# Linear attention into a gated MLP: the first pair's v from GpSimd in half precision, and the sixth tile stored in halves

## The chip, the cores and the metric

The kernel runs on one core of one Trainium2 chip. The metric is the device time of one execution in microseconds (us), lower is better; the time of a kernel is the median of several executions. A profile shows one more execution with the start and length of every instruction. Five instruction streams run side by side on the core: TensorE (PE, matmuls; PEld is its weight load), VectorE (DVE), ScalarE (ACT), GpSimd (POOL) and SyncE (SP). A DMA is issued from one of these streams and carried out by 16 DMA engines that all streams share. In the profile a DMA issued from SP or ACT shows as queue q1 or q10 ("hardware_dynamic") and one issued from POOL as queue q0 ("software_dynamic"). POOL's can convert the type on the way.

## What is computed

A linear attention over 8 batches, 8 heads, 576 rows and 64 columns, an RMS norm per head, and then a two-layer MLP with a sigmoid gate on the 4608 rows of 512:

```python
kv  = np.einsum('bhsd,bhse->bhde', k, v)
out = np.einsum('bhsd,bhde->bhse', q, kv)
rms = np.sqrt(np.mean(out * out, axis=-1, keepdims=True) + 1e-06)
x   = (out / rms * g_norm).transpose(0, 2, 1, 3).reshape(4608, 512)
h   = x @ w_in                                # 512 -> 2048
g   = h * (1.0 / (1.0 + np.exp(-1.702 * h)))
y   = g @ w_out                               # 2048 -> 512
```

Inputs and output are float32. On the chip the matmuls run on float16.

## The kernel before

The 4608 rows go through the MLP as nine tiles of 512: tile t below 8 holds the first 512 rows of batch t, and tile 8 the 64 rows that each batch has over. While the MLP of one tile runs on PE, the attention of a later batch is worked in between. From the second tile on both layers of the MLP are done with seven products where eight would be usual (`SevenIn`, `Seven`), with sums formed on DVE.

Nothing reorders the program: each engine runs its instructions in the order in which the code emits them, and a semaphore wait on the first instruction of a stream holds all that are behind it.

**The opening** is what the change touches. Batch 0 is worked by head pairs c = 0 to 3 (`NPAIR` = 4). A pair has q, k and v of two heads, laid as 96 partitions by 768 values (`early_src`). The first pair is loaded on SP's list in float32 into staging tiles named `qf` (lines 154 to 161: first k, then q, then v) and cast to float16 into `kraw`, `qraw` and `vbuf`: q on ACT (L860), k and v on DVE (L861, L862). Pairs 1 to 3 are loaded on POOL's list by `early_load` (L91), which converts to float16 on the way, nine loads in the order q, k, v per pair (L187 to L189). Behind them on POOL's list stand eight loads of `moe_w_in` by `load_w_in` (L180; lines 190 to 197): three pieces of 512 columns and 128 rows for the first four column blocks, then columns 8 and 9 (in blocks of 128) for all rows, then the fourth piece of the first four blocks, and so on; then `moe_w_out` (L206) and batch 1.

POOL uses eight DMA semaphores in turn (they read DMASW0 to DMASW7 in the listings below; SP's and ACT's are DMAHW0 to DMAHW7). A load on POOL's list can only be issued when the load eight places ahead of it has landed, since it reuses that one's semaphore.

On PE the opening reads: 12 matmuls on zeros (`busy(12)`, L869), the transposes of the first pair's q (L439, `a0.q(0)`), 2 matmuls on zeros, the k-v product of the first pair (L261, `a0.kv(0)`), its output product (L307), and so on pair by pair; L384 is the sum for the norm (`ss`), L325 and L386 are its square and root on ACT, L394 scales on DVE. Then come the first hidden blocks (L478, `d0.mm`): the first four column blocks with rows 0, 1 and 2, then column blocks 8 and 9 with rows 0 to 2, then the fourth row piece for all six.

**The stores.** A finished tile lies in `osbs[t]` (128 partitions, 4 by 512). For the tiles named in `HALVED`, `place` (L696) issues a store from SP for each half when the half is full; tiles 6 and 7 are stored whole at the end of `layers` (L801, `store`, L852). Tile 8 is stored in pieces (L743).

```python
        elif self.t in HALVED and j == 1 - i:
            store(self.t, 2 * i, 2 * i + 2)
```

Of the kernel before, what the change touches and what calls it, by code (L numbers as in the profile page):

```python
# [8 lines left out]
F32 = mybir.dt.float32  # L9
# [3 lines left out]
P = 128  # L13
# [3 lines left out]
def kernel(  # L17
# [10 lines left out]
    nc = tc.nc  # L28
# [14 lines left out]
    PE_ = 96  # L43
# [6 lines left out]
    stage = ctx.enter_context(tc.tile_pool(name="stage", bufs=4))  # L50
# [18 lines left out]
    vbuf = const.tile([P, NPAIR, 2 * NJ * D], F16)  # L69
# [17 lines left out]
    def early_src(n, b, c0, c1):  # L87
        return srcs[n][b, 2 * c0 : 2 * c1].rearrange("h (p j) d -> p h (j d)", j=NJ)

    def early_load(n, b, c0, c1):  # L90
        nc.gpsimd.dma_start(  # L91
            out=raw[n][0:PE_, c0:c1, :].rearrange("p c (l x) -> p (c l) x", l=2),
            in_=early_src(n, b, c0, c1),
        )
# [57 lines left out]
            )  # L152

    first = {}
    for n in "kqv":
        if n != "q":
            rows = stage.tile([P, 6, 2 * P], F32, name="qf", tag="qf", bufs=2)
            rows = rows.rearrange("p h x -> p (h x)")[0:PE_]
        first[n] = rows[:, (n == "q") * 2 * NJ * D :][:, 0 : 2 * NJ * D]
        dst, src = first[n].rearrange("p (h x) -> p h x", h=2), early_src(n, 0, 0, 1)  # L160
        nc.sync.dma_start(out=dst, in_=src)
# [17 lines left out]
    def load_w_in(f0, f1, k0=0, k1=KO):  # L179
# [4 lines left out]
            ),  # L184
        )

    for c in range(1, NPAIR):  # L187
        for n in "qkv":
            early_load(n, 0, c, c + 1)  # L189
# [429 lines left out]
    class Seven:  # L619
# [60 lines left out]
        def place(self, name, mo, with_, i, j):  # L680
# [9 lines left out]
            if self.t == B:  # L690
# [3 lines left out]
                else:  # L694
                    store_rest(2 + mo, j * HN, (j + 1) * HN)
            elif self.t in HALVED and j == 1 - i:  # L696
                store(self.t, 2 * i, 2 * i + 2)
# [34 lines left out]
    def store_rest(mo, n0, n1):  # L732
        osb = osbs[B]
        for g in range(2):
            rows = out[(2 * mo + g) * S : (2 * mo + g + 1) * S, n0:n1]
            if 2 * mo + g < EARLY:
                p0 = SM % PE_
                rows = rows[bass.DynSlice(NJ * p0 + SM // PE_, R, step=NJ), :]
            else:
                rows = rows[SM:S, :]  # L740
            late = mo == 2 and n0 > 0
            queue = nc.gpsimd if mo == 0 or late else (nc.sync, nc.scalar)[g]
            queue.dma_start(out=rows, in_=osb[g * R : (g + 1) * R, mo, n0:n1])  # L743
# [43 lines left out]
    def layers(t, units1, units2):  # L787
# [11 lines left out]
        else:  # L799
            project_all(hid.gT, units2)  # L800
        if EARLY <= t < B and t not in HALVED:  # L801
            store(t, 0, J)
# [11 lines left out]
    def project_all(gT, units):  # L814

        os = {}

        def project(mo, fo):
            if fo == 0:
                pool, tag = (ps_h, "hT") if mo < 2 else (ps_o, "o")  # L820
                os[mo] = pool.tile([P, DM], F32, name="o", tag=tag)
            nc.tensor.matmul(  # L822
                os[mo],
                gT[:, fo, mo * P : (mo + 1) * P],
                w_out_sb[:, fo, :],
                start=(fo == 0),
                stop=(fo == FO - 1),
            )
            if fo == FO - 1:
                copy = nc.scalar.copy if mo % 2 else nc.vector.tensor_copy  # L830
                copy(osbs[0][:, mo, :], os[mo])

        steps = [(mo, 4 * i + k) for i in range(3) for mo in range(4) for k in range(4)]
        steps += [(mo, fo) for fo in (12, 13) for mo in range(4)]
        steps += [(mo, 14 + k) for mo in range(4) for k in range(2)]
        for n, (mo, fo) in enumerate(steps):
            project(mo, fo)
            for u in units.get(n, ()):
                u()
# [11 lines left out]
    def store(t, j0, j1):  # L851
        nc.sync.dma_start(  # L852
            out=out[t * S : t * S + SM, :].rearrange("(p j) m -> p j m", j=J)[:, j0:j1],
            in_=osbs[t][:, j0:j1],
        )
# [3 lines left out]

    nc.scalar.copy(qraw[0:PE_, 0, :], first["q"])  # L860
    nc.vector.tensor_copy(kraw[0:PE_, 0, :], first["k"])  # L861
    nc.vector.tensor_copy(vbuf[0:PE_, 0, :], first["v"])  # L862


    idle_ps = ps_h.tile([P, SM], F32, name="idle", tag="hT")
# [110 lines left out]
    def plan(t):  # L976
        return SECOND if t < EARLY else LATER if t < B - 1 else LAST_TWO

    HALVED = (2, 3, 4, 5)
    live = {0: a0}  # L980

    def start(b):
# [136 lines left out]
```

## Time and profile before

| | before |
|---|---|
| median of 3 executions | 258.72 us (258.68 to 258.73) |
| the profiled execution | 258.06 us |
| its span (first to last instruction) | 256.3 us |
| granted TensorE clock | 0.999 |
| POOL's queue (q0) | 18.31 MB, 37648 packets |
| SP's queue (q1) | 16.29 MB, 30624 packets |

The span is the part of the execution that the profile shows; 1.8 us of the profiled execution lie around it. MB counts what a DMA writes, so a load that converts float32 to float16 reads twice that. A line of the timeline gives the start in us, the length in us, the engine, the line of the code, the operation, output and input, and how many were merged; in brackets stands the idle time before it and what ended it. A line of the chain of waits gives start, length and what ran then. A DMA line of POOL or SP in the timeline is the time of issuing it, and not that of its data.

### The profile page before, as it was taken

What the parts mean: (1) busy time and instruction counts of PE and PEld (TensorE: products, weight loads), DVE (VectorE), ACT (ScalarE), POOL (GpSimd) and SP (SyncE); (2) the same over time, 40 slices, a digit from 0 to 9 for tenths busy, and PEclk for the clock granted to TensorE, in tenths of its full rate; (3) what the DMA queues carried; (4) which work ended last, traced back from release to release, by engine and by line L of the source; (5) the groups of instructions that cost most, each with busy time, mean ns of one, the idle gap of its engine ahead of it and who ended that gap; (6) DMA issues with size and microseconds to landing.
All of it is one profiled execution on the core that took longest, in us unless ns stands there. A gap on an engine that the chain in (4) does not pass through costs nothing.

```text
span 256.3 us, 6351 instructions
## 1 busy us (share of the span) xinstructions
PE 250.1 (98%) x2596; PEld 203.5 (79%) x2596; DVE 194.3 (76%) x341; ACT 176.9 (69%) x322; POOL 57.5 (22%) x94
## 2 busy tenths in 40 slices
PE   8899999999999999999999999999999999999994
PEld 2444544888888888888888888888888888888883
DVE  2557675999958895989588867986799687857872
ACT  3468826978759885988598958895788569537800
POOL 8872255404080103301340143000000000000013
PEclk9999999999999999999999999999999999999999
DMA  7999999999999989998999799909500430012005
GB/s 179 198 199 206 204 203 197 190 173 150 141 163 220 133 118 177 209 271 114 216 170 130 90 232 145 154 4 145 195 4 0 100 148 3 0 75 91 0 22 146
DMA packets 68703, 35.33 MB, mean 138 GB/s; under 512 B 37986, under 2 KB 66274, under 8 KB 68418
## 3 DMA queue, kind: packets, MB, share of 16 engines
q0 software_dynamic: 37648, 18.31, 55.5%
q1 hardware_dynamic: 30624, 16.29, 28.0%
q8 instruction: 20, 0.33, 0.5%
q10 hardware_dynamic: 402, 0.33, 0.4%
q14 instruction: 9, 0.07, 0.1%
HBM read 36.70 MB, written 9.44 MB: 180 GB/s over the span
## 4 chain that ended last, share of the span: by engine, by line
PE 92%; POOL 3%; DMA 3%; issue 0%; DVE 0%
PE o L709 39%; PE h L589 38%; PE o L822 5%; PE hT L478 4%; DMA w_in_sb<-in_moe_w_in_dram 3%; PE kvp L248 2%; PE outR L337 1%; POOL qraw L91 1%; POOL kraw L91 1%; POOL vbuf L91 1%; PE ss L384 1%; POOL w_in_sb L180 1%; PE q L459 0%; PE kvp L261 0%; PE outT L307 0%
## 5 line engine op out<-in xcount | busy, mean ns | idle before, releaser
L566 ACT ACTIVATE gT<-h 128x512 f16<-128x512 f32 x96 | 52.3, 601 | 5.7 <-PE h L589 5.7
L589 PEld LDWEIGHTS <-ws 128*128 128x128 f16 x512 | 50.1, 98 | 5.9
L709 PEld LDWEIGHTS <-gS 128*128 128x128 f16 x512 | 49.0, 98 | 6.2 <-DVE gS L641 0.3
L589 PE MATMUL h<-xS,ws 128*128 128x256 f16 x384 | 52.2, 273 | 0.0
L709 PE MATMUL o<-tw,gS 128*128 128x256 f16 x384 | 45.6, 273 | 0.0
L589 PEld LDWEIGHTS <-w_in_sb 128*128 128x128 f16 x384 | 37.5, 98 | 4.7
L709 PEld LDWEIGHTS <-gT 128*128 128x128 f16 x384 | 37.6, 98 | 4.3
L709 PE MATMUL o<-w_out_sb,gT 128*128 128x256 f16 x256 | 31.4, 273 | 0.0
L589 PE MATMUL h<-xT,w_in_sb 128*128 128x256 f16 x224 | 31.1, 272 | 0.0
L603 DVE TENSOR_TENSOR h<-h,s 128x512 f32<-128x512 f32 x32 | 22.3, 697 | 4.4 <-PE h L589 2.8
L605 DVE TENSOR_TENSOR s<-h,s 128x512 f32<-128x512 f32 x32 | 22.1, 691 | 4.3 <-PE h L589 3.5
L686 DVE TENSOR_TENSOR osb<-o,qf 128x512 f32<-128x512 f32 (+1 forms) x25 | 16.7, 667 | 11.2 <-PE o L709 11.1
L743 POOL DMA_DIRECT2D out_dram<-osb x6 | 3.2, 538 | 93.3 <-DVE osb L686 93.3
L641 DVE TENSOR_TENSOR gS<-gT 128x512 f16<-128x512 f16 (+2 forms) x32 | 21.3, 684 | 0.6 <-ACT gT L566 0.6
L566 ACT ACTIVATE gT<-s 128x512 f16<-128x512 f32 x32 | 19.8, 628 | 2.8 <-DVE s L605 2.8
L535 DVE COPY s<-h 128x512 f32<-128x512 f32 x19 | 13.0, 685 | 8.1 <-PE h L589 8.0
L589 PE MATMUL h<-xS,w_in_sb 128*128 128x256 f16 x128 | 18.9, 273 | 0.0
L353 DVE TENSOR_REDUCE sum<-sq 128x8 f32<-128x512 f16 x24 | 14.9, 678 | 4.7 <-ACT sq L347 4.7
L993 ACT ACT_TABLE_LOAD x14 | 18.0, 1283 | 0.2
L325 ACT ACTIVATE sq<-outT 128x512 f16<-128x512 f32 (+1 forms) x16 | 7.8, 493 | 14.8 <-PE outT L307 9.2
L115 POOL DMA_DIRECT2D kraw<-in_k_dram x7 | 6.0, 855 | 49.2 <-PE kvp L248 32.6
L535 ACT COPY h<-h 128x512 f32<-128x512 f32 x27 | 15.4, 577 | 2.1 <-PE h L589 1.8
(105 smaller groups left out, 365.4 us busy)
## 6 DMA issues: line engine op xcount, KB each, us to landing
out_dram<-osb SPq DMA_DIRECT2D x8, 512.0 KB, 5.6
kraw<-in_k_dram POOLq DMA_DIRECT2D x5, 512.0 KB, 6.1
vbuf<-in_v_dram POOLq DMA_DIRECT2D x5, 512.0 KB, 9.9
out_dram<-osb SPq DMA_DIRECT2D x2, 1024.0 KB, 4.8
qraw<-in_q_dram POOLq DMA_DIRECT2D x3, 512.0 KB, 11.0
qbuf<-in_q_dram POOLq DMA_DIRECT2D x3, 512.0 KB, 12.0
out_dram<-osb SPq DMA_DIRECT2D x6, 192.0 KB, 6.1
w_in_sb<-in_moe_w_in_dram POOLq DMA_DIRECT2D x2, 512.0 KB, 9.9
```

Of the source, the lines that this page charges most:

```text
L353: nc.vector.tensor_reduce(out=self.sum4[:, j, :], in_=self.o[j][1].rearrange("p (x d) -> p x d", d=D), op=ALU.add, axis=mybir.AxisListType.X,)
L478: nc.tensor.matmul(self.h[fo], w_in_sb[:, ko, fo * P : (fo + 1) * P], self.x[:, ko], start=(ko == 0), stop=(ko == KO - 1),)
L535: (nc.vector.tensor_copy if engine == "D" else nc.scalar.copy)(to, src)
L566: nc.scalar.activation(self.gT[:, to, n * TH : (n + 1) * TH], src, AFT.Gelu_apprx_sigmoid)
L589: nc.tensor.matmul(bank[name][:, a], w, x, start=(p in (1, 5) and a == 0 and k == 0), stop=(k == KH - 1), skip_group_check=True,)
L603: nc.vector.tensor_add(bank["z"], bank["x"], self.s5)
L605: nc.vector.tensor_add(self.s5, bank["x"], self.s5)
L641: op(s[:, n, lo], a, b)
L686: nc.vector.tensor_add(o, ps, self.kept[with_][:, m])
L709: nc.tensor.matmul(o, a, w, start=(p in (1, 2, 5) and i == 0 and (mo == 0 or split)), stop=(i == HF - 1), skip_group_check=True,)
L822: nc.tensor.matmul(os[mo], gT[:, fo, mo * P : (mo + 1) * P], w_out_sb[:, fo, :], start=(fo == 0), stop=(fo == FO - 1),)
L993: u2.setdefault(i, []).append(lambda: f(*args))
```

## The change

The first pair's v leaves SP's list and the float32 staging tile. It becomes the first load on POOL's list, which writes float16 straight into `vbuf`. The cast on DVE falls away. SP's list begins with two loads, k and q. All that stood on POOL's list stands one place further back. Apart from that, tile 6 joins the tiles that are stored in halves.

```diff
     first = {}
-    for n in "kqv":
-        if n != "q":
-            rows = stage.tile([P, 6, 2 * P], F32, name="qf", tag="qf", bufs=2)
-            rows = rows.rearrange("p h x -> p (h x)")[0:PE_]
+    rows = stage.tile([P, 6, 2 * P], F32, name="qf", tag="qf", bufs=2)
+    rows = rows.rearrange("p h x -> p (h x)")[0:PE_]
+    for n in "kq":
         first[n] = rows[:, (n == "q") * 2 * NJ * D :][:, 0 : 2 * NJ * D]
...
+    early_load("v", 0, 0, 1)
     for c in range(1, NPAIR):
         for n in "qkv":
             early_load(n, 0, c, c + 1)
...
     nc.vector.tensor_copy(kraw[0:PE_, 0, :], first["k"])
-    nc.vector.tensor_copy(vbuf[0:PE_, 0, :], first["v"])
...
-    HALVED = (2, 3, 4, 5)
+    HALVED = (2, 3, 4, 5, 6)
```

POOL's list from its first DMA to the first load of `moe_w_in`, before (the brackets name the semaphore that the instruction waits for):

```order
L91 DMA qraw<-in_q_dram 96x2x384
L91 DMA kraw<-in_k_dram 96x2x384
L91 DMA vbuf<-in_v_dram 96x2x384
L91 DMA qraw<-in_q_dram 96x2x384
L91 DMA kraw<-in_k_dram 96x2x384
L91 DMA vbuf<-in_v_dram 96x2x384
L91 DMA qraw<-in_q_dram 96x2x384
L91 DMA kraw<-in_k_dram 96x2x384
L91 DMA vbuf<-in_v_dram 96x2x384 [waits DMASW0_49]
L180 DMA w_in_sb<-in_moe_w_in_dram 128x512 [waits DMASW1_49]
```

The same place with the change:

```order
L91 DMA vbuf<-in_v_dram 96x2x384
L91 DMA qraw<-in_q_dram 96x2x384
L91 DMA kraw<-in_k_dram 96x2x384
L91 DMA vbuf<-in_v_dram 96x2x384
L91 DMA qraw<-in_q_dram 96x2x384
L91 DMA kraw<-in_k_dram 96x2x384
L91 DMA vbuf<-in_v_dram 96x2x384
L91 DMA qraw<-in_q_dram 96x2x384
L91 DMA kraw<-in_k_dram 96x2x384 [waits DMASW0_49]
L91 DMA vbuf<-in_v_dram 96x2x384 [waits DMASW1_49]
L179 DMA w_in_sb<-in_moe_w_in_dram 128x512 [waits DMASW2_49]
```

Each load has moved one place back and one semaphore on, so the load that it waits for is the same as before; the only new wait is that of the third pair's k for the new first load.

The end of SP's list, where the stores of tiles 6 and 7 stand behind the last transposes (the `x` in the names is the normed attention output of batch 7):

```order
-L373 DMA_TRANSPOSE xT<-x_3174 128x8x128 x2
-L852 DMA out_dram<-osb 128x2048 x2
+L373 DMA_TRANSPOSE xT<-x_3172 128x8x128 x2
+L852 DMA out_dram<-osb 128x1024 x2
+L852 DMA out_dram<-osb 128x2048
 L743 DMA out_dram<-osb 64x256 x5
```

One of the two whole stores has become two half stores; behind them stands what stood there before.

## The prediction

> **What bounds the kernel now.** I read the page first, then the chain of waits, then the timeline of the opening, and last the DMA queues in short windows.
>
> ```profile
> PE 250.1 (98%) x2596; PEld 203.5 (79%) x2596; DVE 194.3 (76%) x341; ACT 176.9 (69%) x322; POOL 57.5 (22%) x94
> PE 92%; POOL 3%; DMA 3%; issue 0%; DVE 0%
> ```
>
> PE is busy nearly all the span and makes up 92% of the chain that ended last. The change leaves PE's list as it is, so it can only move the moment from which PE runs without a gap. The chain in order of time shows that moment:
>
> ```profile
> 1.84 0.73 POOL qraw L91
> ...
> 6.99 0.62 POOL vbuf L91
> ...
> 9.85 6.81 DMA w_in_sb<-in_moe_w_in_dram
> 16.66 0.05 issue
> 16.70 4.49 PE hT L478 x20
> 21.20 0.12 PE outT L419 x4
> 21.31 6.91 PE hT L478 x32
> 28.22 1.08 PE o L822 x5
> ```
>
> From 16.70 us on it is PE without a break. Ahead of that stands one load of `moe_w_in`, columns 8 and 9, issued at 9.85 and landed at 16.66. The timeline shows who waits in the opening:
>
> ```profile
> 5.96 0.79 DVE L862 CAST vbuf<-qf 96x768 f16<-96x768 f32 x1 [1.09 <-DMA qf<-in_v_dram]
> 7.43 0.38 PE L261 MATMUL kv<-vbuf,kraw 96*64 96x64 f16 x12
> 11.74 0.45 PE L439 MATMUL q<-ident,qraw 96*64 96x96 f16 x12
> 12.09 0.59 ACT L325 ACTIVATE sq<-outT 128x512 f16<-128x512 f32 x1
> 12.68 0.38 PE L261 MATMUL kv<-vbuf,kraw 96*64 96x64 f16 x12 [0.50 <-DMA vbuf<-in_v_dram]
> 12.99 0.39 PE L384 MATMUL ss<-sq,ones 128*128 128x512 f16 x1
> 16.70 4.49 PE L478 MATMUL hT<-xT,w_in_sb 128*128 128x512 f16 x20 [0.25 <-DMA w_in_sb<-in_moe_w_in_dram]
> ```
>
> PE stands 0.50 us for the last pair's v and 0.25 us for columns 8 and 9. Both come through POOL's queue, so PE follows that queue: what shifts the queue shifts the end. That leaves the question of what paces the queue, issuing or data:
>
> ```profile
> 1.79 0.79 POOL L91 DMA_DIRECT2D qraw<-in_q_dram  x1
> qraw<-in_q_dram POOLq DMA_DIRECT2D x1, 144.0 KB, 4.8
> 6.92 0.69 POOL L91 DMA_DIRECT2D vbuf<-in_v_dram  x1
> vbuf<-in_v_dram POOLq DMA_DIRECT2D x1, 144.0 KB, 5.6
> GB/s 0 0 0 59 194 344 341 283 277 264 203 171 198 194 191 192 191 198 200 198 198 201 201 201 200 201 199 190 221 185 204 189 192 197 202 203 206 209 207 203
> ```
>
> The last number of a DMA row is the time from issue to landing. The first of POOL's nine loads lands at 1.79 + 4.8 = 6.6, the ninth at 6.92 + 5.6 = 12.5. They were issued (6.92 - 1.79) / 8 = 0.64 us apart and landed 5.9 / 8 = 0.74 apart, so the data set the pace. The row of GB/s cuts 0 to 20 us into 40 slices: from 2.5 us there is no slice in which the engines rest. The chain blames POOL's issuing for the time before 9.85, but its issues there run ahead of the data.
>
> **The change part by part.** *The first pair's v on the other queue.* Its data cost DMA time in either place. The queues in windows, in this order: 0 to 20 us (q1 alone), 1.6 to 4.0, 2.6 to 4.6, 4.0 to 5.2 (two rows), 6 to 12:
>
> ```profile
> q1 hardware_dynamic: 624, 0.88, 15.4%
> q1 hardware_dynamic: 422, 0.61, 88.5%
> q1 hardware_dynamic: 439, 0.62, 104.1%
> q1 hardware_dynamic: 199, 0.27, 78.9%
> q0 software_dynamic: 51, 0.04, 24.5%
> q0 software_dynamic: 1654, 1.18, 130.1%
> ```
>
> SP's three loads are 624 packets, 208 each. By 4.0 us 422 have gone, which is k and q; v fills most of 4.0 to 5.2. No packet of POOL's queue is seen in 1.6 to 4.0, nor up to 4.6; 51 go beside v's before 5.2, and from then POOL has the engines alone at 1654 / 6 = 276 packets per us. The 51 are worth 0.185 us, so POOL's queue stands as if it had begun at full pace at 5.015.
>
> With the change SP's data are through at about 4.0. POOL's queue has one more load; taking the same 208 packets, it costs 208 / 276 = 0.755 us (the spacing of landings above, 0.74, agrees). In float32 on SP's queue a load cost 208 / (439 / 2) = 0.95 us, and v in its own stretch 1.03 (1.2 less 0.185, rounded). If POOL's queue starts as soon as SP's is through, the next load begins at 4.0 + 0.755 = 4.755 in place of 5.015: everything behind is **0.26 us earlier**. With the mean of 0.95 for v it would be 0.19; both are the same step. From what start the sign turns: 5.015 - 0.755 = 4.26 us.
>
> Can the queue start at 4.0? Its first load is issued at 1.79, as the first of the changed list will be. Two other places bound the delay between issue and first packet, one with a quiet q1 and one with a busy one:
>
> ```profile
> 140.76 0.91 POOL L115 DMA_DIRECT2D kraw<-in_k_dram  x1 [9.80 <-PE kvp L248]
> q0 software_dynamic: 282, 0.14, 76.6%
> 98.71 0.88 POOL L115 DMA_DIRECT2D vbuf<-in_v_dram  x1
> q1 hardware_dynamic: 1343, 0.45, 108.8%
> q0 software_dynamic: 69, 0.04, 39.2%
> ```
>
> The first q0 row is 142 to 144 us (from 140.8 to 142 q0 has no row): the quiet delay is about 1.3 us. The other two are 98.7 to 101, where q1 alone moves data, and 101 to 102: behind a busy q1 the delay is over 2.3. In the opening it was 2.8 (1.79 to 4.6), q1 being busy all along. With 1.3 from the quiet place POOL could start at 3.1, before SP's two loads are through. I take 4.0 because the late starts go with a busy q1 at both places. As bounds I keep both ends: 4.65, if the start stays where it is, and, for the best, 4.0 with a faster mix, priced below.
>
> [...]
>
> *One more issue on POOL.* Each later load is issued one place later, about 0.64 us. It is hidden by the lag of 4.8 to 5.6 us between issue and landing, of which 1.3 is the quiet delay and 0.75 the load's own data. The wait for the load eight places ahead is unchanged. The one new wait, the third pair's k for the new first load, asks at about 6.9 for something landed by 6.3 at worst (next step).
>
> *The first pair's v itself.* Sent by 4.76, or by 5.4 from a start at 4.65. The first POOL load of before had its 208 packets out at about 5.2 + (208 - 51) / 276 = 5.8 and landed at 6.6, so 0.8 on top: 5.6 to 6.2. PE wants it at 7.43, behind the zero matmuls and q's transposes: at least 1.2 us of cover, cost nothing. Were the cover gone, PE would stand for the excess.
>
> *The cast on DVE* (0.79 us, 5.96 to 6.75) goes. Nothing on DVE behind it was late: its next work waits for PE, and k-v began at 7.43 by PE's own order. Worth nothing. SP's third issue goes too, and nothing behind it on SP's list belongs to the opening.
>
> *Tile 6 in halves.*
>
> ```profile
> 201.76 0.69 DVE L686 TENSOR_TENSOR osb<-o,qf 128x512 f32<-128x512 f32 x1 [0.66 <-PE o L709]
> 203.50 0.58 ACT L689 COPY osb<-o 128x512 f32<-128x512 f32 x1 [2.26 <-PE o L709]
> 204.11 25.01 SPq L852 DMA_DIRECT2D out_dram<-osb  x2
> 202.00:204.00 2.00, 2.00 (x21) 1.80 (x19) 1.45 (x4) 0.50 (x2) 0.00 (x0) 1.00 0.00 0
> ```
>
> The first half can leave at 202.5 in place of 204.1. In 202 to 204 the DMA share is 0.00, the transposes ahead on SP are over, and the next thing on SP is tile 7's store some 25 us later. Worth nothing.
>
> *From the queue to the end.* 0.26 earlier reaches the last pair's v (PE is free at 11.74 + 0.45 = 12.19, so up to 0.49 can be used), the norm sum at 12.99 (its square on ACT ends at 12.68: 0.31), and the wait at 16.70. Every later piece of `moe_w_in` moves with the same queue, and PE runs on unbroken. So the sum is -0.26: the profiled execution would go from 258.06 to 257.80. The median shown is 0.66 above that execution; I carry the difference over: 258.72 - 0.26 = **258.46**.
>
> **The rivals.**
>
> *The start stays at 4.65* (slower). POOL's first DMA needs 2.8 us by itself, whatever q1 does. From 4.65 to 5.2 the queue then sends 0.55 x 276 = 152 packets where 51 went before, and has 208 more to send: (208 - 101) / 276 = +0.39, **259.11**. It decides from any start after 4.26. For it: in 1.6 to 4.6 not one q0 packet is seen though the quiet delay would allow 3.1. Against it: 140.76.
>
> *Issuing is the bound* (slower). If the chain's reading is right and POOL's issues pace the queue, a further issue moves all by its length, 0.62 to 0.73 us in the chain: about +0.62, **259.34**. Against it: landings 0.74 apart from issues 0.64 apart. It decides if the lag from issue to landing falls to about 2.05 us.
>
> *More than v's share is saved* (faster). The slices show 344 and 341 GB/s at 2.5 to 3.5 us, then 283 and 277. If three float32 loads in flight cause the drop, k and q keep the first pace of 342: the 0.14 MB of 3.5 to 4.0 takes 0.41 in place of 0.5, and the mix with POOL's lighter writes may begin before 4.0, at 3.1; at POOL's read rate (twice 197 GB/s written) the 0.26 MB of 3.1 to 4.0 takes 0.66 in place of 0.9. Together up to 0.33 more: -0.59. PE can use 0.31 + 0.25 = 0.56 of it: **258.16**.
>
> *The change does not do what it says* isn't open: the order shows v leaving SP's list and PE waiting on POOL's load.
>
> **How the numbers follow.** -0.26 with 0.52, of it 0.07 beyond -0.52; more saved 0.20, of it 0.13 beyond; start unmoved 0.18, of it 0.06 beyond +0.52; issue-bound 0.10, of it 0.08 beyond. A measurement of this kernel tells some 0.2%, 0.52 us, from no change. So faster 0.07 + 0.13 = 0.20, slower 0.06 + 0.08 = 0.14, same 0.66. The likeliest case's own range is 258.25 to 258.65 (0.2 either way for the start and v's price). To leave out no more than 2 in 10 the range reaches to 258.1 and to 259.2, which drops the issue-bound case and the tails of the other two.
>
> **What would show it.** Right: q0 packets from about 4.0, the last pair's v awaited until about 12.4, columns 8 and 9 landing near 16.4, PE unbroken from there, and PE's wait on the first v not visible. Wrong: no q0 packet before 4.6 and PE's start near 17.1 (first rival), or landings 0.6 later with idle DMA slices (second). Any change past 30 us other than a plain shift would mean that something I hold to be hidden is not.

## The result, and the profile after

The changed kernel takes 260.91 us (median of 6 executions, 260.48 to 261.33) where the kernel before takes 258.70 us beside it (6 executions, 258.28 to 259.96). The ratio is 1.0087, with a 95% interval of 1.0064 to 1.0109: slower by some 2.2 us, where 0.26 us faster was forecast and the range ended at 259.2. The profiled execution took 260.58 us, its span is 258.8 us.

Busy time, the granted clock in 40 slices and the shares of the chain of waits, from the page of the kernel after:

```profile
PE 251.7 (97%) x2596; PEld 204.5 (79%) x2596; DVE 193.3 (75%) x340; ACT 176.9 (68%) x322; POOL 58.2 (22%) x95
PEclk9869999999999999999999999999999999999999
PE 94%; DMA 2%; POOL 2%; DVE 0%; issue 0%
```

PE still has the same 2596 matmuls and still sets the end. The new thing is the second row: its second and third slices, 6.5 to 19.4 us, read 8 and 6. The clock was not full there. The chain in order of time, after (start, length, what ran):

```profile
5.80 5.60 DMA vbuf<-in_v_dram
11.40 0.14 issue
11.54 0.53 PE kv L261 x12
...
17.81 0.25 PE ss L384
18.06 5.61 PE hT L478 x26
23.67 0.12 PE outT L419 x4
23.79 6.91 PE hT L478 x32
30.69 1.08 PE o L822 x5
```

The last three rows have their partners in the chain of before at 21.20, 21.31 and 28.22: everything is 2.47 to 2.48 us later, and the pieces themselves are as long as they were. (The medians differ by only 2.2 us, since the profiled execution of before, 258.06 us, was a quick one.) So the whole loss is made before 23.67 us. The chain no longer passes through columns 8 and 9 of `moe_w_in`, but through the third pair's v, issued at 5.80, and from there PE has work without a break. That work is slow. PE in the opening, from the timeline of after:

```profile
7.56 0.38 PE L307 MATMUL outT<-qT,kvb 128*128 128x512 f16 x1
9.03 0.38 PE L261 MATMUL kv<-vbuf,kraw 96*64 96x64 f16 x12 [0.72 <-DMA vbuf<-in_v_dram]
11.54 0.53 PE L261 MATMUL kv<-vbuf,kraw 96*64 96x64 f16 x12 [0.97 <-DMA vbuf<-in_v_dram]
15.89 1.91 PE L478 MATMUL hT<-xT,w_in_sb 128*128 128x512 f16 x4
```

PE now stands 0.72 us for the second pair's v and 0.97 us for the third's, waits that before did not have. From 11.54 on the same matmuls take longer: four of line 478 take 1.91 us, and 1.03 us before. The windows show why (length, busy time of PE, PEld, DVE, ACT, POOL, then granted clock, DMA share, GB/s); after:

```profile
10.00:11.00 1.00, 0.56 (x13) 0.31 (x12) 0.40 (x1) 0.94 (x2) 0.59 (x2) 0.96 1.28 187
11.00:12.00 1.00, 0.47 (x13) 0.43 (x13) 0.06 (x1) 0.00 (x0) 1.00 (x2) 0.50 1.28 196
15.00:17.00 2.00, 2.00 (x6) 0.71 (x5) 0.79 (x2) 1.14 (x2) 1.96 (x3) 0.50 1.42 199
17.00:18.00 1.00, 1.00 (x4) 0.40 (x3) 0.00 (x0) 0.00 (x0) 0.12 (x2) 0.62 1.39 180
7.60:11.00 3.40, 2.18 (x40) 1.11 (x38) 1.15 (x3) 1.77 (x3) 2.44 (x6) 0.99 1.28 188
```

The same long window, before:

```profile
7.60:11.00 3.40, 3.06 (x69) 1.82 (x64) 1.30 (x5) 1.73 (x3) 2.81 (x6) 1.00 1.30 197
```

In the 3.4 us up to 11.0 PE was busy for 2.18 us, before for 3.06. Then the granted clock is 0.50, from 10.92 (0.96 in its second) to 17.76 (0.62 in its): 6.84 us of matmuls at half rate.

The other half of the story is POOL's queue. Its packets after, in the windows 3.4 to 4.0, 5.2 to 8, 8 to 12 and 0 to 12 us:

```profile
q0 software_dynamic: 12, 0.01, 12.6%
q0 software_dynamic: 648, 0.46, 121.2%
q0 software_dynamic: 1077, 0.77, 129.2%
q0 software_dynamic: 1924, 1.37, 82.9%
```

And before, in 5.2 to 8, 8 to 12 and 0 to 12:

```profile
q0 software_dynamic: 741, 0.53, 128.6%
q0 software_dynamic: 1111, 0.79, 130.2%
q0 software_dynamic: 1903, 1.36, 75.8%
```

The queue does start earlier, just before 4.0 as forecast. But by 12 us it has sent 1924 packets where it had sent 1903 before, and 208 of the 1924 are the new load's. What everything else on the queue has got by 12 us is down from 1903 to 1716. The issue of columns 8 and 9, the first of the two in this row of the timeline of after:

```profile
10.93 1.28 POOL L179 DMA_DIRECT2D w_in_sb<-in_moe_w_in_dram  x2 [0.23 <-DMA kraw<-in_k_dram]
```

And the view of the DMA issues for that stretch, after, whose last number is the time to landing:

```profile
w_in_sb<-in_moe_w_in_dram POOLq DMA_DIRECT2D x1, 256.0 KB, 6.4
```

They land at 10.93 + 6.4 = 17.3, 0.7 later than the 16.66 of before. They are also issued 1.08 us later, and only 0.66 of that is there at the first load of `moe_w_in` (8.29 against 7.63). From then on POOL waits 0.28, 0.45 and 0.23 us for the landing of earlier loads whose semaphores it reuses. PE, at half clock, does not even wait for them: it comes by at 17.81.

So there are two losses to tell apart: a queue that is 0.7 us late, and a clock that is halved for 6.84 us.

### The profile page after: what moved, and what is told of

The parts are those of the page before. It is cut to its first block, busy times and chain, and to the rows that moved or that the text cites. A ratio compares the mean times of both kernels' runs of the same rounds, so it can differ in the third digit from the quotient of the medians.

```text
span 258.8 us, 6347 instructions
## 1 busy us (share of the span) xinstructions
PE 251.7 (97%) x2596; PEld 204.5 (79%) x2596; DVE 193.3 (75%) x340; ACT 176.9 (68%) x322; POOL 58.2 (22%) x95
## 4 chain that ended last, share of the span: by engine, by line
PE 94%; DMA 2%; POOL 2%; DVE 0%; issue 0%
PE o L709 38%; PE h L589 38%; PE hT L478 6%; PE o L822 5%; DMA vbuf<-in_v_dram 2%; PE kvp L248 2%; PE outR L337 1%; PE ss L384 1%; PE outT L307 1%; POOL vbuf L91 1%; POOL qraw L91 0%; POOL kraw L91 0%; PE kv L261 0%; PE q L459 0%; PE kvp L261 0%; PE outT L311 0%
## 5 line engine op out<-in xcount | busy, mean ns | idle before, releaser
L386 ACT ACTIVATE rs<-ss,eps_t 128x512 f32<-128x512 f32 (+1 forms) x16 | 9.2, 580 | 13.5 <-PE ss L384 13.5
```

## The experiments

Times are medians; the ratio is against the kernel before on the same chip, with its 95% interval. Each execution also gives its mean granted clock over the span. It reads 0.997 to 1.000 where the clock stayed up in the opening, and 0.980 to 0.993 where it fell (0.950 in one execution of before).

**1. Which part of the change.** The changed kernel with tile 6 whole again, and the kernel before with tile 6 in halves.

```diff
-    HALVED = (2, 3, 4, 5, 6)
+    HALVED = (2, 3, 4, 5)
```

> The changed kernel with tile 6 stored whole again, so only v's move is left. Theory (v's move in the opening did it): +2.2 us against before, as the whole change; the granted clock at 0.50 from about 11 to 17.6 us. Rival (the halves of tile 6 cost something at the tail): clearly less than +2.2.

> The kernel before with tile 6 stored in halves and nothing else. Theory: no difference to before (within 0.3 us). Rival: it carries a part of the +2.2 us.

The v alone: 260.87 us, ratio 1.0077 (1.0050 to 1.0105). The halves alone: 258.68 us, ratio 1.0006 (0.9983 to 1.0030). The move of v carries the loss, the halves are worth nothing that can be seen. Nine of the ten executions with v moved had a clock of 0.984 to 0.993 and took 259.69 to 262.04; the one whose clock stayed at 1.000 took 259.50. That one, 0.9 over the 258.56 of before, is a single value for the loss without the clock. The kernel before, beside them, has executions of both kinds too: 27 with the clock up have a median of 258.50, and three at 0.993 took 259.65 to 260.23.

**2. Keep the clock up.** The changed kernel with seven zero matmuls in PE's two waits.

```diff
     a0.q(1)
+    busy(3)
     a0.kv(1)
     a0.ss(0)
     a0.out(1)
+    busy(4)
     a0.q(2)
```

> The changed kernel with three more matmuls on zeros ahead of the second pair's k-v product and four ahead of the third pair's q transposes, about 0.65 and 0.86 us at full clock, in stretches in which PE waited for loads. Theory A (the waits let the granted clock fall to 0.50 and the half clock is most of the loss): the clock stays at 1.00, and the loss shrinks from +2.2 to the lateness of columns 8 and 9, about +0.7 us. Theory B (the late loads are the loss, the half clock runs beside them): no gain, still about +2.2, or more by what the added matmuls take.

259.31 us, ratio 1.0021 (0.9998 to 1.0044); no clock under 0.997 in ten executions. PE in the long window, from the windows of this kernel:

```profile
7.60:11.00 3.40, 3.33 (x50) 1.67 (x50) 1.13 (x5) 0.87 (x2) 2.49 (x5) 1.00 1.24 177
```

And the wait that is left, from its timeline:

```profile
17.50 1.69 PE L478 MATMUL hT<-xT,w_in_sb 128*128 128x512 f16 x7 [0.28 <-DMA w_in_sb<-in_moe_w_in_dram]
```

More work on PE made the kernel 1.56 us faster than the change alone (260.87 to 259.31, both beside the same runs of before). The clock is the larger loss, and it falls because PE has gaps: with them it was at 0.987 to 0.993 in all six executions of the changed kernel, with zero matmuls in them at 0.997 or more in all ten. Some 0.75 us remain. In the profiled execution PE waits for `moe_w_in`; what the zero matmuls themselves cost is left to experiment 9.

**3. One more load and nothing else.** The kernel before, v still on SP, with one more load of the same 208 packets, into a tile that nobody reads, ahead of POOL's nine.

```diff
+    spare = const.tile([P, 2 * NJ * D], F16, name="spare")
+    nc.gpsimd.dma_start(
+        out=spare[0:PE_].rearrange("p (l x) -> p l x", l=2), in_=early_src("v", 0, 0, 1)
+    )
     for c in range(1, NPAIR):
```

> The kernel before (v on SP's list, cast on DVE) with one more load of the same kind at the head of POOL's list into a buffer that nobody reads, so POOL's loads are late without v having moved. Theory A: everything on the queue 0.75 us later, so at least +0.75; where PE's waits get long enough for the clock to fall, +1.5 to +2.5. Theory C (POOL's queue is slow because it starts while nothing else is left to send, a matter of v's absence from SP's list): POOL's pace after 5.2 us is the 275 packets per us of before, and the loss is +0.75 at most.

259.62 us, ratio 1.0047 (1.0017 to 1.0076). Four executions had a clock of 0.984 to 0.993 and took 260.34 to 262.00; the six others took 258.85 to 259.74, their median 259.08 being 0.5 over the 258.56 of all executions of before. The profiled execution is one of these six. Its timeline:

```profile
11.24 0.38 PE L265 MATMUL kv<-vbuf,kraw 96*64 96x64 f16 x12 [0.56 <-DMA vbuf<-in_v_dram]
13.46 0.38 PE L265 MATMUL kv<-vbuf,kraw 96*64 96x64 f16 x12 [0.69 <-DMA vbuf<-in_v_dram]
17.46 1.90 PE L482 MATMUL hT<-xT,w_in_sb 128*128 128x512 f16 x8 [0.19 <-DMA w_in_sb<-in_moe_w_in_dram]
```

Its q0 packets in 0 to 12 us, from the DMA queues:

```profile
q0 software_dynamic: 1911, 1.36, 75.4%
```

And PE's second block in its chain of waits:

```profile
22.07 6.96 PE hT L482 x32
```

Here SP sent three loads and in the changed kernel two, and yet POOL's queue had sent 1911 packets against 1924. Its pace in 5.2 to 8 us was 743 / 2.8 = 265 packets per us, that of before, as theory C had it. The block that began at 21.31 before begins at 22.07: 0.76 us late, close to the 0.755 that the prediction gave to 208 packets. One pair of executions can't measure that, though: in the profiled execution of experiment 5, whose POOL list and time are those of before, PE's wait for columns 8 and 9 ended at 17.57, 0.87 later than in that of before (16.70), and here it ended at 17.46. The medians with the clock up are the better measure: 259.08 against 258.50, so the load costs some 0.6 us. In the changed kernel, where SP is relieved of its own, it costs no less as far as the one execution of experiment 1 with the clock up can say (0.9).

**4. Is it POOL's late start?** The first four loads of the changed kernel ahead of POOL's mask and constants, and the same with the first three loads in the kernel before.

```diff
     nc.vector.memset(kvb[1], 0.0)
+    early_load("v", 0, 0, 1)
+    for n in "qkv":
+        early_load(n, 0, 1, 2)
     nc.gpsimd.affine_select(
...
-    early_load("v", 0, 0, 1)
-    for c in range(1, NPAIR):
+    for c in range(2, NPAIR):
```

> The changed kernel with POOL's first four loads (first pair's v, second pair's q, k, v) ahead of POOL's masks and memsets, so its first issue is at about 0.8 us in place of 1.8. Theory D (POOL's queue runs slowly in 4 to 8 us, 224 packets per us in place of 275, because it has few loads waiting when SP's data end): with a deeper backlog the pace in 5.2 to 8 us rises towards 270 and the loss falls from +2.2 to between -0.3 and +0.5 us; the clock stays at 1.00. Rival E (the pace is slow because the first pair's v is missing on SP's list, whatever the backlog): the pace in 5.2 to 8 us stays near 225, and the loss falls by at most the earlier start.

> The kernel before with POOL's first three loads ahead of its masks and memsets. Theory (the engines are busy with SP's three loads until 5.2 us and the queue has backlog anyway): within 0.3 us of before. Rival (POOL's earlier packets push back SP's q and v and with them PE's start, or the queue gains 0.5 us): more than 0.3 us either way.

In the changed kernel 261.70 us, ratio 1.0112 (1.0077 to 1.0146), the clock down in all four executions. In the kernel before 259.04 us, ratio 1.0028 (0.9991 to 1.0065), the clock down in three of ten. The gain expected of the first did not come. The second is 0.37 over the 258.67 beside it, with an interval that holds no change, so it decides nothing. POOL's queue in the first, in 5.2 to 8 and 8 to 12 us:

```profile
q0 software_dynamic: 757, 0.54, 129.2%
q0 software_dynamic: 891, 0.63, 119.5%
```

Two windows of it:

```profile
9.00:10.00 1.00, 0.84 (x14) 0.41 (x13) 0.14 (x2) 0.88 (x2) 1.00 (x3) 1.00 1.05 128
10.00:11.00 1.00, 0.00 (x0) 0.00 (x0) 0.40 (x1) 0.29 (x1) 1.00 (x3) 1.00 1.21 151
```

And PE's wait in the timeline of the second:

```profile
8.19 0.38 PE L263 MATMUL kv<-vbuf,kraw 96*64 96x64 f16 x12 [1.65 <-DVE vbuf L864]
```

An early start of the queue was not kept. In the first kernel the loads were issued from 1.34 us (0.8 was expected), and the pace in 5.2 to 8 us did rise to 757 / 2.8 = 270, as theory D had it and rival E had not: by 8 us 1009 packets were sent, in the changed kernel 847. But POOL's masks and memsets now stand behind the fourth load, the fifth is issued at 5.12 in place of 4.56, and in 8 to 12 us the pace is 891 / 4 = 223. The DMA share dips to 1.05 at 9 to 10 us, and PE has no matmul at all in 10 to 11. In the second SP's v comes late instead: issued at 1.70 it takes 5.8 us to land, so its cast on DVE begins at 7.50 where it began at 5.96 before, and the first k-v product waits 1.65 us for that.

**5. Is SP's order the matter?** The kernel before, with v's float32 load issued by ACT.

```diff
-        nc.sync.dma_start(out=dst, in_=src)
+        (nc.scalar if n == "v" else nc.sync).dma_start(out=dst, in_=src)
```

> The kernel before with the first pair's v in float32 on ACT's list in place of SP's, cast on DVE as before; POOL's list unchanged. Theory D: v still fills the engines until 5 us while POOL's backlog builds, pace in 5.2 to 8 us near 270, time within 0.3 us of before. Rival E (it is SP's shorter list): pace near 225 and a loss.

258.68 us, ratio 0.9993 (0.9976 to 1.0009): no difference. The pace in 5.2 to 8 us was 739 / 2.8 = 264. Whether SP or ACT issued the float32 load did not matter here.

**6. Gaps without late data.** The kernel before without the two pairs of zero matmuls behind q's transposes and behind the first k-v.

```diff
     a0.q(0)
-    busy(2)
     a0.kv(0)
...
-    busy(2)
     a0.out(0)
```

> The kernel before without the two pairs of matmuls on zeros behind the first q transposes and behind the first k-v product; no DMA is touched. Theory A (PE's idle share ahead of 11 us sets the granted clock): PE gets emptier in 6.5 to 11 us, the clock falls to 0.50 in some or all executions, and those are 1 to 2 us slower, the others equal to before. Theory B (only late loads cost): no difference.

259.50 us, ratio 1.0026 (0.9996 to 1.0056). Seven of ten executions had a clock of 0.985 to 0.993, where the kernel before beside it had 5 of 26. The profiled execution is one of the three others, with PE busy for 2.25 of the 3.40 us, close to the 2.18 of the changed kernel:

```profile
7.60:11.00 3.40, 2.25 (x46) 1.30 (x48) 1.37 (x5) 1.77 (x3) 2.62 (x5) 1.00 1.30 196
```

So gaps on PE make the fall frequent, though the data are those of before; that busy share alone does not decide each execution. Nor does every fall cost: two of the seven, at 0.993, took 258.52 and 258.67, the time of before.

**7. No first v at all.** The changed kernel without any load of the first pair's v.

```diff
-    early_load("v", 0, 0, 1)
...
-                        vbuf[0:PE_, c, x],
+                        (vbuf if c or self.b else kraw)[0:PE_, c, x],
```

> The changed kernel without any load of the first pair's v: POOL's list has its nine loads of before, SP's list two, and the first pair's k stands in for v, so that product is not the reference's. Theory F (POOL's queue has a pace of its own in the opening, some 1850 to 1920 packets by 12 us whatever SP sends): columns 8 and 9 land near 16.6 as before, and the time is within 0.4 us of before. Rival (the engine time freed on SP's queue goes to POOL's, as the forecast had it): the queue 0.8 to 1.0 us earlier, 2150 packets or more by 12 us, time 0.4 us or more below before.

259.98 us, ratio 1.0033 (1.0005 to 1.0061), in two groups: four executions with a clock of 0.999 or 1.000 took 258.38 to 258.65, six with 0.984 to 0.993 took 259.74 to 260.89. The profiled execution is one of the six. Its q0 packets in 0 to 12 us:

```profile
q0 software_dynamic: 1795, 1.28, 78.1%
```

A wait of PE in its timeline:

```profile
11.08 0.53 PE L260 MATMUL kv<-vbuf,kraw 96*64 96x64 f16 x12 [0.88 <-DMA vbuf<-in_v_dram]
```

The long window, and the ones in which its clock falls and comes back:

```profile
7.60:11.00 3.40, 2.26 (x40) 1.12 (x39) 1.21 (x3) 1.77 (x3) 2.29 (x5) 1.00 1.19 172
11.00:12.00 1.00, 0.92 (x13) 0.53 (x14) 0.35 (x2) 0.00 (x0) 0.82 (x3) 0.54 1.31 200
17.00:18.00 1.00, 1.00 (x5) 0.30 (x3) 0.00 (x0) 0.10 (x1) 0.80 (x2) 0.55 1.36 197
```

And the second block in its chain of waits:

```profile
23.67 6.91 PE hT L477 x32
```

This is the plainest run on the forecast's main term. SP sends a third less, POOL has no load to take it over, and POOL's queue has sent 1795 packets by 12 us, not more than the 1903 of before and fewer than the 1850 of theory F. Columns 8 and 9 land at 10.53 + 6.1 = 16.6, as before. Where the clock stays up, the time is that of before; nothing is gained. Where it falls, the second block begins at 23.67 in place of 21.31, 2.36 us later, with no packet added. Within this one kernel the six executions with the clock down took 1.9 us more than the four with it up (medians 260.50 and 258.58). The clock alone is enough for nearly the whole loss.

**8. Fewer constants on POOL.** The three memsets of `ones2` go from POOL to DVE, in the kernel before and in the changed kernel with the zero matmuls of 2.

```diff
-    nc.gpsimd.memset(ones2, 0.0)
-    nc.gpsimd.memset(ones2[0:D, 0:D], 1.0)
-    nc.gpsimd.memset(ones2[D:P, D:P], 1.0)
...
+    nc.vector.memset(ones2, 0.0)
+    nc.vector.memset(ones2[0:D, 0:D], 1.0)
+    nc.vector.memset(ones2[D:P, D:P], 1.0)
```

> The kernel before with the three memsets of the ones mask on DVE, so that POOL issues its first load at about 1.3 us in place of 1.79. Theory F: the whole queue up to 0.5 us earlier, columns 8 and 9 near 16.2, time 0.2 to 0.5 us below before. Rival (the 16 engines bound the queue, as with SP's three loads until 5.2 us): no difference, within 0.2 us.

> The changed kernel with the seven added matmuls on zeros and with the three memsets of the ones mask on DVE. Theory F with theory A: POOL's first issue about 0.5 us earlier takes back two thirds of the added load, clock at 1.00, time +0.2 to +0.5 us against before, in place of +0.75 with the matmuls alone. Rival: +0.75 as without.

In the kernel before 258.69 us, ratio 0.9986 (0.9967 to 1.0005). In the changed kernel 259.28 us, ratio 1.0019 (0.9997 to 1.0041), no better than without it. Neither beats the kernel before, and the gain that theory F expected of each did not come; POOL's first load was issued at 1.49 and 1.50, 0.3 earlier and not 0.5. The first has the lowest ratio of all, but its interval holds no change. Its clock fell in none of ten executions, that of the kernel before beside it in 6 of 25, which may be all there is to it: with the clock up the medians are 258.70 and 258.49.

**9. No first v, and the zero matmuls.** Experiment 7 with the seven zero matmuls of 2.

> The kernel without any load of the first pair's v (k stands in for v in that pair, so the values of that pair are not the reference's), with the same seven zero matmuls that the earlier run put in PE's waits (three ahead of the second pair's k-v, four ahead of the third pair's q transposes). Without the fills its ten runs fell into two groups: 258.38 to 258.65 at a granted clock of 0.999 or 1.000, and 259.74 to 260.89 at 0.984 to 0.993. Theory A (the clock is what separates the groups, and PE's gaps at 8 to 12 us are what lets it fall): all or nearly all runs at 0.997 or more, median 258.3 to 258.8, the time of the kernel before, since columns 8 and 9 land where they do there. Then the fills in the changed kernel left 259.3 only because of the 208 added packets. Rival (the fills themselves cost what was left in the changed kernel, because they push PE's own list back): clock at 1.00 too, but 259.1 to 259.5. Rival (the clock falls for another reason than PE's gaps): two groups again, median 259.5 to 260.5.

259.06 us, ratio 1.0022 (1.0006 to 1.0037); no clock under 0.997 in twelve executions, where without the zero matmuls six of ten were. The rival of another cause for the fall is out. But the time is 0.26 over theory A's range, and 0.74 over the 258.32 of before beside it, which bears out the rival that the zero matmuls cost time of their own. Seven executions at 1.000 took 258.43 to 259.06, with a median of 258.78, 0.46 over before; the five at 0.997 and 0.998 took 259.31 to 259.48, and why they differ isn't known, since none of them was profiled. The profiled execution is the fastest, 258.43 us. In it no wait of PE between 5 and 23 us is for a load; it comes to its second block by its own list. Its timeline:

```profile
15.81 3.40 PE L477 MATMUL hT<-xT,w_in_sb 128*128 128x512 f16 x15
```

And its chain of waits:

```profile
21.70 6.91 PE hT L477 x32
```

21.70 against 21.31: 0.39 later, with no packet added. So the 0.75 us left in experiment 2 can't be put down to the late queue; the zero matmuls may be most of it. What the late queue costs is taken from experiment 3, which has no added matmul, and from the one execution of experiment 1 whose clock stayed up.

How often the clock was under 0.995, with PE's busy time in 7.60 to 11.00 us of the one profiled execution:

| kernel | clock down | PE busy of 3.40 us |
|---|---|---|
| before (beside experiments 1 to 9) | 16 of 99 | 3.06 |
| after | 6 of 6 | 2.18 |
| 1, v alone | 9 of 10 | 2.40 |
| 1, halves alone | 2 of 10 | 3.08 |
| 2, after with zero matmuls | 0 of 10 | 3.33 |
| 3, before with one more load | 4 of 10 | 2.95 |
| 4, after with loads first | 4 of 4 | 2.22 |
| 4, before with loads first | 3 of 10 | 2.62 |
| 5, v on ACT's list | 0 of 10 | 3.21 |
| 6, before without zero matmuls | 7 of 10 | 2.25 |
| 7, no first v | 6 of 10 | 2.26 |
| 8, before, constants on DVE | 0 of 10 | 2.90 |
| 8, after with zero matmuls, constants on DVE | 0 of 10 | 3.33 |
| 9, no first v, zero matmuls | 0 of 12 | 3.33 |

## Why the prediction was wrong

*The bound was read rightly, and only halfway.* PE follows POOL's queue, and past the opening there is nothing but a shift: that held. But the argument took PE's waits as time lost once. It had no term for what a wait does to the clock, and the granted clock stood in the profile of before as 1.00 in every window up to 240 us, so no row asked for it. One length might have: the first twelve zero matmuls took 5.30 us, 0.44 each, where the twenty of line 478 at 16.70 took 4.49 / 20 = 0.22 each, and the granted clock reads 1.00 for both.

*The start at about 4.0 held.* The first q0 packets are seen in 3.4 to 4.0 us; the rival of a start that stays at 4.65 is out.

*The step that failed* is the one behind it: from 4.0 the queue was to run at 276 packets per us, so that "the next load begins at 4.0 + 0.755 = 4.755 in place of 5.015". That pace would have given (12 - 4.0) x 276 = 2208 packets by 12 us; there were 1924. In 5.2 to 8 us it ran at 648 / 2.8 = 231 per us, before at 741 / 2.8 = 265, with fewer bytes beside it on SP's queue. The prediction read 276 from a stretch that the queue reaches after some time, and held SP's v to be what had kept it from there. In truth SP's v took next to nothing from POOL: with it (1903), without it (1795 in experiment 7), or with it and one more load on POOL (1911), POOL's queue sends 1795 to 1911 packets by 12 us. The stretch that v left free was used, 199 packets by 5.2 us against 51 before, and then lost again, 93 fewer in 5.2 to 8 and 34 fewer in 8 to 12. So the term for the time freed on SP, which the prediction gives as 1.03 us (1.2 less 0.185 is 1.015), was about 0: with no load of v at all, experiment 7 took 258.58 with its clock up, and before 258.49. The 208 packets on POOL stood alone, at a price of 0.755; experiment 3 measured some 0.6 by its medians, and columns 8 and 9 in the changed kernel landed 0.7 late.

*The step that was missing* is larger. The late queue, and a PE that got to its second pair earlier (7.56 us at `outT` against 8.39), together made waits of 0.72 and 0.97 us. In the second of them the clock fell to 0.50, and it stayed there for 6.84 us. With the clock held by zero matmuls, the change is 0.75 us slower, without them 2.2; the difference of some 1.5 us is the clock's, and more by what the zero matmuls cost (the same kernel with its clock up and down differs by 1.9 in experiment 7). The two losses do not add up: at half clock PE comes to columns 8 and 9 after they have landed, so the late queue costs nothing of its own there, and where the clock fell without any late queue the block was 2.36 us late, against 2.48 in the changed kernel.

*What held:* the first v had cover (no wait at the first k-v product after the change), but little of the 1.2 us, as PE was there at 6.60 and not at 7.43; in the profile of experiment 1 PE waits 0.16 us for it. The two halves of tile 6 were worth nothing (the second run of experiment 1); the cast on DVE was not measured by itself. The one new wait, that of the last pair's k ("the third pair's" above, counted without the first), cost nothing: it was issued at 7.04 without a gap. But the waits for the load eight places ahead, which the prediction called unchanged, grew with the later landings, to the 0.28, 0.45 and 0.23 us above. The lag from issue to landing did not fall towards the 2.05 us that the prediction took as the mark of issuing as the bound; its medians for the loads issued up to 11 us are 5.3 to 6.4. The rivals on the slower side name 259.11 and 259.34, near the 259.3 to 259.5 of the changed kernel with its clock up, but that is luck: the first one's late start did not come, and nothing shows the second one's mechanism.

*What stays open.* Why POOL's queue is slower from 5.2 to 8 us with two float32 loads beside it than with three. With three (on SP, or on SP and ACT) it ran at 260 to 265 packets per us in four profiled executions (before, experiments 3, 5 and 6) and at 228 in a fifth (experiment 8); with two at 196 to 231 in five (after, v alone in experiment 1, experiments 2 and 7, the second kernel of 8), and at 270 with four loads issued ahead of the masks (experiment 4). (The other kernel of experiment 4 is left out, since there 117 of SP's own packets reach into that stretch.) So too few loads waiting when SP's data end is the likelier reason. It is argued and not shown: the 270 is one execution, and the 228 speaks against it.

Why PE reached `outT` 0.83 us earlier in the profiled execution has to do with its first zero matmuls. Before and after:

```profile
1.28 5.30 PE L869 MATMUL idle<-kvb 128*128 128x512 f16 x12 [1.28 <-DVE one_t L202]
1.28 4.14 PE L868 MATMUL idle<-kvb 128*128 128x512 f16 x12 [1.28 <-DVE one_t L202]
```

Long and short ones occur with v on SP and with v on POOL, so it isn't the edit alone. In the four profiled executions whose clock fell the twelve took 4.14 to 4.31 us, in the ten others 4.23 to 5.30. That hints at a link with the falling clock, but the two ranges overlap.

## What to carry to other kernels

Ahead of moving a transfer from one DMA queue to another, count how many packets the receiving queue had sent by the time that matters; time freed on the other queue is a gain only if a run shows the receiving queue speeding up when its neighbour is quiet, and here it did not (1795 packets by 12 us without v, 1903 with it). Where PE waits in short gaps, look at the granted clock in windows of a few us and at its mean over several executions: here the clock fell in the second of two gaps of 0.72 and 0.97 us and stayed at 0.50 for 6.84 us, and seven matmuls on zeros in them brought back 1.56 us of a loss of some 2.3. Such matmuls stand in PE's own order and cost time of their own once nothing is late, 0.4 to 0.7 us for seven of them here. And one profiled execution is one sample: with the same list on POOL, PE's wait for one load ended 0.87 us apart in two of them.

## What the runs showed of the hardware

The clock fell to 0.50 with no gap between matmuls longer than 0.97 us in the timeline of after, with PE busy 2.18 us of the 3.40 ahead. It stayed down for 6.84 us there, and in experiment 7 from 11.08 (0.54 in its second) to 17.90 (0.55): 6.82 us. The two other profiled executions whose clock fell, read the same way, give 6.82 us (v alone in experiment 1, 11.28 to 18.10) and 6.84 us (the first kernel of experiment 4, 11.06 to 17.90, behind a gap of 1.70 us). So the length is nearly the same in all four, and no run shows what sets it. The mean clock tells as much: 6.84 us at half clock take 0.013 off the mean of a span of 258.8 us, which gives the 0.987 of that execution. By the same sum the many executions at 0.993 had about half as long a stretch, an estimate, since none of them was profiled. Why the same kernel falls in some executions and not in others, no run here shows either. PE was busy for 6.16 of the 6.84 us of the low stretch of after, and from 11.54 on, 0.62 us into it, it had work, which did not bring the clock back for another 6.2 us.

POOL's queue came out much the same whatever SP's queue did: 1795 to 1931 packets by 12 us in all fourteen profiled executions, with three float32 loads on SP or two, and with one load more or none on POOL. Loads issued earlier were ahead at 8 us and no longer at 12 (experiment 4).
